# A two-layer sliding-window transformer on one core: ring, banks, masks and GLU halves rearranged

## The chip, the cores and the metric

The kernel runs on one core of one Trainium2 chip. The metric is the time of one execution on the device in microseconds; three runs of the kernel before gave a median of 736.29 us (734.07 to 737.18).

## The reference

Two layers, each of attention and a gated unit, on 2048 tokens of width 512, in bf16:

```python
x = x + A_ref(layernorm(x))     # 32 heads of 16; query i sees keys j with 0 <= i - j < 256; then @ wo
x = x + B_ref(layernorm(x))     # (sigmoid(x @ w_gate) * (x @ w_up)) @ w_down, inner width 1792
x = x + A_ref(layernorm(x))     # the same weights again
x = x + B_ref(layernorm(x))
```

## The kernel before

Tokens go in 16 tiles of 128 and 4 groups of 512. The program is fully unrolled and every engine works in the order in which it was issued. `run` (L364) writes that order: 256 slots of the attention (layer, key tile `t`, head group `g` of 4 heads, eight slots a tile), and into each slot it fills other work up to a budget `T_SLOT` of estimated TensorE nanoseconds.

A slot issues, in order: `scores` (L275), four matmuls side by side of one key tile against the three query tiles that can see it, into the one score tile of four PSUM banks, and one exponential on ScalarE into a ring in SBUF; every fourth slot `values` (L304), 48 small matmuls for one query tile and 16 heads, five slots after the first scores that it needs; the steps that have come due (`at`, L357); units of the streams; and last `mask` (L293), a multiply on VectorE for the diagonal block and a select on GpSimd for the block at the window's end. A step that follows another comes one slot later: values, two transposes with the division between them (`norm1`, `norm2`), output product (`oproj`) with the residual and the layer norm's statistics, normalising (`ln_apply`), its transpose (`ln_transpose`). All these transposes use one PSUM bank, `ps_m`; the 512-wide products use the two banks of `ps_d`.

Streams are lists of units: projections (`proj_units`, 12 units of four matmuls of 512 columns for each group) and GLU (`glu_units`, 28 such units for gate and up and 12 pieces of the down product). A unit may run when the group's four tiles are normalised and transposed, and for projections 3 and up from a free slot (L360: 58, 90, 122, 154, 186) on, since keys and values have three buffers. GLU streams go one after the other. A down product of layer 0 starts a layer norm for layer 1. GLU weights come by DMA in chunks of 128 columns, three buffers deep.

Before slot 0 the first four tiles are normalised and the whole of projection group 0 runs. `Vaug` holds each head's 16 values and a one (the sum of the softmax) at stride 18; GpSimd clears it at the start.

Of the kernel before, what the change touches and what calls it, by code (L numbers as in the profile page):

```python
# [23 lines left out]
RING_SLOTS = 7  # L24
_RING_PS = [(0, 1), (3, 1), (0, 3)]
# [7 lines left out]
T_SLOT = 2050  # L33


def ring_ps(j):
    return _RING_PS[j % 3]


def ring_slot(j, b):  # L40
    p, s = ring_ps(j)
    return p + b * s


class Net:
# [3 lines left out]
    def __init__(self, ctx, tc, A_x, wqkv, wo, w_gate, w_up, w_down, out):  # L49
# [11 lines left out]
        self.ln_st = pool("ln_st", 4)  # L61
        self.ln_xn = pool("ln_xn", 4)
        self.xnp = pool("xn_t", 3)
        self.ktp = pool("kt_tmp", 1)
# [17 lines left out]
        self.ring = big.tile([P, H, RING_SLOTS, P], BF16, name="PTring")  # L82

# [8 lines left out]
        nc.sync.dma_start(out=self.wot[:], in_=wo.rearrange("(k p) m -> p k m", p=P))  # L92
        nc.sync.dma_start(out=self.wd[:], in_=w_down.rearrange("(c p) m -> p c m", p=P))

        self.ident = big.tile([P, P], BF16, name="ident")
# [3 lines left out]
        self.nhalf = big.tile([P, 1], F32, name="nhalf")  # L99
        nc.gpsimd.memset(self.nhalf[:], -0.5)  # L100
        self.rms = [big.tile([P, 1], F32, name=f"rm{e}") for e in range(2)]
        nc.vector.memset(self.rms[0][:], 0.0)
        for m in range(4):
# [3 lines left out]
        self.maskq = big.tile([P, 4, P], BF16, name="maskq")  # L107
        nc.gpsimd.memset(self.maskq[:], 1.0)
        nc.gpsimd.affine_select(out=self.maskq[:], in_=self.maskq[:], compare_op=ALU.is_ge, fill=0.0,
                                base=0, pattern=[[0, 4], [1, P]], channel_multiplier=-1)  # L110
        for i in range(3):
            nc.gpsimd.memset(self.Vaug[i][:], 0.0)
            onesv = self.Vaug[i][:, :, 0:VS * H].rearrange("p t (h c) -> p t h c", c=VS)[:, :, :, 16:17]
            nc.gpsimd.memset(onesv, 1.0)

        self.ready = set()
        self.due = []
        self.xn = {}
# [3 lines left out]
        self.chunk_next = 0  # L122

    def ln_stats(self, key, t):
# [6 lines left out]
        nc.gpsimd.tensor_scalar(out=rs[:, 0:1], in0=mv[:, 1:2], scalar1=1e-5, scalar2=None, op0=ALU.add)  # L133
# [11 lines left out]
    def ln_later(self, key, t, first=0):  # L145

        if first:
            self.at(first, 0, lambda: self.ln_stats(key, t))
        else:
            self.ln_stats(key, t)  # L150
        self.at(first + 1, 0, lambda: self.ln_apply(key, t))
        self.at(first + 2, KT * T_TR, lambda: self.ln_transpose(key, t))

    def ln_transpose(self, key, t, bank=None):
        nc = self.nc
        tt = t % NBG
        if tt == 0:
            self.xnT[key] = self.xnp.tile([P, KT, TGW], BF16, name="xnT")
        xn = self.xn.pop((key, t))
        pt = (bank or self.ps_m).tile([P, KT, P], BF16, name="ln_tp", tag="d" if bank else "m")  # L160
        for c in range(KT):
            nc.tensor.transpose(pt[:, c, :], xn[:, c * P:(c + 1) * P], self.ident[:])  # L162
        nc.vector.tensor_copy(out=self.xnT[key][:, :, tt * P:(tt + 1) * P], in_=pt[:])  # L163
        if tt == NBG - 1:
            self.ready.add(key)
# [3 lines left out]
    def proj_units(self, L, tg):  # L169
        key = ("p", L, tg)  # L170
        b = (L * NTG + tg) % 3
        units = []
        for which in (1, 0):
            for cq in range(NCQ):
                units.append((KT * T_MM, lambda which=which, cq=cq: self._qk(key, tg, b, which, cq)))
        for tt in range(NBG):
            units.append((KT * T_MM, lambda tt=tt: self._v(key, tg, b, tt)))
        return units

    def _qk(self, key, tg, b, which, cq):  # L180
# [10 lines left out]
        if cq == 0:  # L191
            self.kt = self.ktp.tile([P, NCQ, TGW], BF16, name="kt")
        nc.scalar.copy(out=self.kt[:, cq, :], in_=pt[:])  # L193
        for e in range(2):
            nc.vector.tensor_scalar(out=self.kTp[b][:, cq, e, :], in0=self.kt[:, cq, :],
                                    scalar1=self.rms[e][:, 0:1], scalar2=None, op0=ALU.mult)
# [13 lines left out]
    def glu_units(self, L, tg):  # L210
        key = ("g", L, tg)
        units = []
        for fc in range(FC):
            units.append((KT * T_MM, lambda fc=fc: self._gate(key, L, tg, fc)))
            units.append((KT * T_MM, lambda fc=fc: self._up(key, L, tg, fc)))
        cuts = [0, 5, 10, FC]
        for tt in range(NBG):
            for a, b in zip(cuts, cuts[1:]):
                units.append(((b - a) * T_MM, lambda tt=tt, a=a, b=b: self._down(L, tg, tt, a, b)))
        return units  # L220

    def load_chunk(self):
        i = self.chunk_next
        if i >= NGI * FC:
            return
        self.chunk_next += 1
        fc = i % FC
        w = self.wgup.tile([P, KT, 2, P], BF16, name="wgu")
        self.nc.sync.dma_start(out=w[:, :, 0, :], in_=self.wg_src[:, :, fc * P:(fc + 1) * P])
        self.nc.sync.dma_start(out=w[:, :, 1, :], in_=self.wu_src[:, :, fc * P:(fc + 1) * P])  # L230
        self.chunk_w[i] = w

    def _gate(self, key, L, tg, fc):
# [12 lines left out]
    def _up(self, key, L, tg, fc):
        nc = self.nc
        w = self.chunk_w.pop((L * NTG + tg) * FC + fc)
        xnT = self.xnT[key]
        ps = self.ps_d.tile([P, TGW], F32, name="ups", tag="d")  # L250
        for kt in range(KT):
            nc.tensor.matmul(ps[:], lhsT=w[:, kt, 1, :], rhs=xnT[:, kt, :], start=(kt == 0), stop=(kt == KT - 1))  # L252
        nc.vector.scalar_tensor_tensor(out=self.hT[:, fc, :], in0=self.th[:], scalar=1.0, in1=ps[:],  # L253
                                       op0=ALU.add, op1=ALU.mult)
        if fc == FC - 1:
            del self.xnT[key]

    def _down(self, L, tg, tt, a, b):
        nc = self.nc
        t = tg * NBG + tt  # L260
# [5 lines left out]
        if b == FC:  # L266
            nc.vector.tensor_tensor(out=self.xsb[:, t, :], in0=self.xsb[:, t, :], in1=self.dps[:], op=ALU.add)
            if L == 0:
                self.ln_later(("p", 1, tg), t)
# [5 lines left out]
    def scores(self, L, t, g):  # L275
# [4 lines left out]
        pj, sj = ring_ps(t)  # L280
        kTp = self.kTp[(L * NTG + t // NBG) % 3]
        ko = (t % NBG) * P
        sps = self.ps_s.tile([P, 4, 512], F32, name="Sps")
        for m in range(4):
            nc.tensor.matmul(sps[:, m, 0:N], lhsT=kTp[32 * m:32 * m + 32, cq, e, ko:ko + P],  # L285
                             rhs=self.qT[32 * m:32 * m + 32, cq, t * P:t * P + N],
                             start=True, stop=True, tile_position=(32 * m, 0))
        h0 = 8 * cq + e
        nc.scalar.activation(out=self.ring[:, h0:h0 + 7:2, pj:pj + (nb - 1) * sj + 1:sj, :],  # L289
# [200 lines left out]
```

## Time and profile before

| | |
|---|---|
| median of 3 runs | 736.29 us |
| the profiled execution | 737.87 us |
| its span, first to last instruction | 736.1 us |
| TensorE matmuls busy, mean granted clock | 85%, 0.942 |
| VectorE, ScalarE, GpSimd busy | 62%, 62%, 30% |

The time of the profiled execution is its span and 1.8 us around it. Busy time is that of all instructions of an engine; a matmul's end is modelled. The granted clock is a share of 2.4 GHz; 0.50 is the lower level, 1.2 GHz. A stretch's mean clock tells how much of it was spent at either. In the rows PE is TensorE's matmuls, PEld its weight loads, DVE VectorE, ACT ScalarE, POOL GpSimd, and in rows of stretches they stand in this order.

### The profile page before, as it was taken

How to read it: one execution, taken by the hardware profiler on the slowest of the kernel's cores; microseconds unless marked ns; L12 is line 12 of the kernel's file. 1: busy time of each engine (PE TensorE's matmuls, PEld its weight loads, DVE VectorE, ACT ScalarE, POOL GpSimd, SP SyncE). 2: the span in 40 equal slices, each digit the busy share in tenths (PEclk: the TensorE clock that was granted, in tenths of full speed). 3: DMA queues.
4: the chain of work that ended last, by engine and by line, in shares of the span. 5: the costliest groups of instructions: out<-in, count | busy, mean ns of one | idle time of the engine just before them, and what ended most of it. 6: DMA issues, size and time to landing. Idle time of an engine off the chain costs nothing.

```text
span 736.1 us, 15556 instructions
## 1 busy us (share of the span) xinstructions
PE 628.3 (85%) x6400; PEld 281.4 (38%) x6400; DVE 459.1 (62%) x1015; ACT 456.5 (62%) x465; POOL 219.5 (30%) x367
## 2 busy tenths in 40 slices
PE   1777866998788998798897899878999999999998
PEld 1233333443333444344333344333444444444443
DVE  3376765576487767667577567758577677665232
ACT  0657866676756787455866687737877677542130
POOL 6144433233343334310233333324333333000000
PEclk9959955899999999899999899979999999999999
DMA  9300000331002311022120203200132043135260
GB/s 293 78 2 1 1 2 1 71 87 45 1 2 58 87 31 29 2 58 59 42 46 2 45 8 89 64 1 2 43 89 59 31 100 88 29 81 121 72 144 29
DMA packets 126727, 38.49 MB, mean 52 GB/s; under 512 B 118720, under 2 KB 126656, under 8 KB 126656
## 3 DMA queue, kind: packets, MB, share of 16 engines
q1 hardware_dynamic: 126656, 37.50, 21.3%
q8 instruction: 50, 0.82, 0.5%
q14 instruction: 21, 0.17, 0.1%
HBM read 35.39 MB, written 2.10 MB: 51 GB/s over the span
## 4 chain that ended last, share of the span: by engine, by line
PE 63%; DVE 21%; ACT 8%; POOL 4%; issue 3%; ACTq 0%; POOLq 0%
PE ups L252 12%; PE gps L242 12%; PE dps L264 12%; ACT PTring L289 7%; PE Sps L285 7%; PE proj_ps L186 5%; DVE ln_stats L131 4%; PE OPps L350 4%; PE OTps L314 3%; DVE xn L141 3%; DVE PTring L298 3%; PE tps L326 3%; DVE xnT L163 3%; DVE xsb L352 2%; POOL ln_rs L134 2%
## 5 line engine op out<-in xcount | busy, mean ns | idle before, releaser
L289 ACT ACTIVATE PTring<-Sps 128x1536 bf16<-128x1536 f32 (+2 forms) x256 | 351.4, 1373 | 123.0 <-PE Sps L285 105.8
L301 POOL TENSOR_SCALAR_AFFINE_SELECT PTring<-PTring 128x512 bf16<-128x512 bf16 x224 | 156.6, 708 | 229.9 <-ACT PTring L289 229.9
L298 DVE TENSOR_TENSOR PTring<-PTring,maskq 128x512 bf16<-128x512 bf16 x256 | 123.0, 481 | 36.2 <-ACT PTring L289 35.8
L253 DVE SCALAR_TENSOR_TENSOR hT<-gth,ups 128x512 bf16<-128x512 bf16 x112 | 76.8, 685 | 77.7 <-PE ups L252 60.4
L244 ACT ACTIVATE gth<-gps 128x512 bf16<-128x512 f32 x112 | 66.7, 596 | 83.4 <-PE gps L242 81.0
L252 PE MATMUL ups<-xnT,wgu 128*128 128x512 bf16 x448 | 117.5, 385 | 0.5 <-DVE hT L253 0.5
L242 PE MATMUL gps<-xnT,wgu 128*128 128x512 bf16 x448 | 117.0, 384 | 0.0
L264 PE MATMUL dps<-wd,hT 128*128 128x512 bf16 x448 | 112.3, 393 | 0.0
L285 PE MATMUL Sps<-qT,kTp 32*128 32x384 bf16 (+2 forms) x1024 | 89.6, 338 | 20.7 <-ACT PTring L289 20.5
L133 POOL TENSOR_SCALAR ln_rs<-ln_mv 128x1 f32<-128x1 f32 x64 | 18.4, 287 | 218.3 <-DVE ln_mv L132 218.3
L285 PEld LDWEIGHTS <-kTp 32*128 32x128 bf16 x1024 | 30.5, 91 | 129.2 <-issue 128.9
L186 PE MATMUL proj_ps<-xnT,wq 128*128 128x512 bf16 x256 | 67.5, 402 | 3.4 <-ACT kt L193 1.9
L162 PE MATMUL ln_tp<-ident,xn 128*128 128x128 bf16 x256 | 28.7, 242 | 45.7 <-DVE xn L141 39.9
L264 PEld LDWEIGHTS <-hT 128*128 128x128 bf16 x448 | 42.3, 101 | 45.7 <-issue 5.2
L252 PEld LDWEIGHTS <-wgu 128*128 128x128 bf16 x448 | 40.5, 99 | 48.0 <-issue 9.2
L319 DVE CAST OTs<-OTps 128x512 bf16<-128x512 f32 x64 | 44.1, 689 | 23.4 <-PE OTps L314 23.2
L242 PEld LDWEIGHTS <-wgu 128*128 128x128 bf16 x448 | 41.7, 99 | 43.4 <-issue 2.5
L314 PE MATMUL OTps<-PTring,Vaug 128*32 128x128 bf16 x2880 | 54.6, 227 | 0.0
L326 PE MATMUL tps<-ident,OTs 128*128 128x128 bf16 x256 | 26.7, 231 | 26.4 <-DVE xnT L163 26.1
L314 PEld LDWEIGHTS <-Vaug 128*32 128x32 bf16 x2880 | 43.0, 100 | 11.5 <-issue 10.4
L141 DVE TENSOR_SCALAR xn<-xsb,ln_mv,ln_rs 128x512 bf16<-128x512 bf16 x64 | 38.2, 601 | 12.8 <-POOL ln_rs L134 11.3
L131 DVE BATCH_NORM_STATS2 ln_stats<-xsb 128x6 f32<-128x512 bf16 x64 | 44.2, 691 | 3.1 <-DMA xsb<-in_A_x_dram 1.5
(37 smaller groups left out, 449.1 us busy)
## 6 DMA issues: line engine op xcount, KB each, us to landing
wgu<-in_B_w_gate_dram SPq DMA_DIRECT2D x112, 128.0 KB, 2.4
wgu<-in_B_w_up_dram SPq DMA_DIRECT2D x112, 128.0 KB, 2.8
out_dram<-xsb SPq DMA_DIRECT2D x16, 128.0 KB, 1.7
wd<-in_B_w_down_dram SPq DMA_DIRECT2D x1, 1792.0 KB, 12.6
wq<-in_A_wqkv_dram SPq DMA_DIRECT2D x3, 512.0 KB, 5.6
xsb<-in_A_x_dram SPq DMA_DIRECT2D x3, 512.0 KB, 8.4
xsb<-in_A_x_dram SPq DMA_DIRECT2D x4, 128.0 KB, 2.3
wot<-in_A_wo_dram SPq DMA_DIRECT2D x1, 512.0 KB, 8.6
```

Source lines behind the costliest of these rows:

```text
L131: nc.vector.bn_stats(out=st[:], in_=self.xsb[:, t, :])
L186: nc.tensor.matmul(pt[:], lhsT=self.wq[:, kt, c0:c0 + P], rhs=xnT[:, kt, :], start=(kt == 0), stop=(kt == KT - 1))
L242: nc.tensor.matmul(ps[:], lhsT=w[:, kt, 0, :], rhs=xnT[:, kt, :], start=(kt == 0), stop=(kt == KT - 1))
L244: nc.scalar.activation(out=self.th[:], in_=ps[:], func=AF.Tanh, scale=0.5)
L252: nc.tensor.matmul(ps[:], lhsT=w[:, kt, 1, :], rhs=xnT[:, kt, :], start=(kt == 0), stop=(kt == KT - 1))
L253: nc.vector.scalar_tensor_tensor(out=self.hT[:, fc, :], in0=self.th[:], scalar=1.0, in1=ps[:], op0=ALU.add, op1=ALU.mult)
L264: nc.tensor.matmul(self.dps[:], lhsT=self.hT[:, fc, tt * P:(tt + 1) * P], rhs=self.wd[:, fc, :], start=(fc == 0), stop=(fc == FC - 1))
L285: nc.tensor.matmul(sps[:, m, 0:N], lhsT=kTp[32 * m:32 * m + 32, cq, e, ko:ko + P], rhs=self.qT[32 * m:32 * m + 32, cq, t * P:t * P + N], s ...
L289: nc.scalar.activation(out=self.ring[:, h0:h0 + 7:2, pj:pj + (nb - 1) * sj + 1:sj, :], in_=sps[:, :, 0:N].rearrange("p w (b c) -> p w b c" ...
L298: nc.vector.tensor_tensor(out=r0, in0=r0, in1=self.maskq[:], op=ALU.mult)
L301: nc.gpsimd.affine_select(out=r2, in_=r2, compare_op=ALU.is_ge, fill=0.0, base=-1, pattern=[[0, 4], [-1, P]], channel_multiplier=1)
L314: nc.tensor.matmul(OT[32 * g:32 * g + 32, col, :], lhsT=Va[:, jj % NBG, VS * h:VS * h + 32], rhs=self.ring[:, h, ring_slot(jj, t - jj), :] ...
```

## The change

- The ring has six blocks instead of seven, by a table. Where the blocks of a key tile lie in the ring in another order than the queries, `scores` issues its matmuls in pieces, so that the exponential still writes one stepped block: one piece for every third key tile, two for the next, three for the third.
- `ps_m` is gone. `ps_d` has three banks, and all transposes take one of them; the score tile is allocated once.
- Values come six slots after the first scores that they need. Masks work on eight heads, every second slot, for the two slots before, and are issued after the slot's first unit.
- The GLU of the first group of layer 0 and of the last group of layer 1 runs as two streams of 256 tokens. A stream now needs its own tiles only. Weight chunks have 256 columns.
- K and Q products are issued in pairs, and a slot asks only for the pair that it needs (`ensure`); what it pulls in counts in the budget. Before slot 0 only the first pair runs. The budget is 2100.
- The epsilon of the layer norm is added on VectorE. K's weights are loaded before Q's; the clears of `Vaug`, now without the value columns, come after the first normalisation.

```diff
-RING_SLOTS = 7
-_RING_PS = [(0, 1), (3, 1), (0, 3)]
+RING_SLOTS = 6
+RING = [(2, 3, 1), (4, 2, 0), (3, 4, 5)]
-T_SLOT = 2050
+T_SLOT = 2100
+LN_DMA = False
...
 def ring_slot(j, b):
-    p, s = ring_ps(j)
-    return p + b * s
+    return RING[j % 3][b]
...
-        self.ktp = pool("kt_tmp", 1)
+        self.ktp = pool("kt_tmp", 2)
...
-        self.ps_s = pool("ps_s", 1, True)
+        ps_fix = pool("ps_fix", 1, True)
         self.ps_o = pool("ps_o", 1, True)
-        self.ps_d = pool("ps_d", 2, True)
-        self.ps_m = pool("ps_m", 1, True)
+        self.ps_d = pool("ps_d", 3, True)
+        self.sps = ps_fix.tile([P, 4, 512], F32, name="Sps")
...
-        for i in range(3):
+        for i in (1, 0, 2):
             nc.sync.dma_start(out=self.wq[:, :, i * D:(i + 1) * D], in_=wq_src[:, :, i * D:(i + 1) * D])
...
+    def constants(self):
+        nc = self.nc
+        for i in range(3):
+            ones = self.Vaug[i][:, :, 0:VS * H].rearrange("p t (h c) -> p t h c", c=VS)[:, :, :, 16:VS]
+            nc.gpsimd.memset(ones, 1.0)
+            nc.gpsimd.memset(self.Vaug[i][:, :, VS * H:VW], 0.0)
+            if i == 0:
+                nc.gpsimd.memset(self.maskq[:], 1.0)
...
-        nc.gpsimd.tensor_scalar(out=rs[:, 0:1], in0=mv[:, 1:2], scalar1=1e-5, scalar2=None, op0=ALU.add)
+        nc.vector.tensor_scalar(out=rs[:, 0:1], in0=mv[:, 1:2], scalar1=1e-5, scalar2=None, op0=ALU.add)
...
+            pt = self.ps_d.tile([P, KT, P], BF16, name="ln_tp", tag="d")
+            for c in range(KT):
+                nc.tensor.transpose(pt[:, c, :], xn[:, c * P:(c + 1) * P], self.ident[:])
+            nc.vector.tensor_copy(out=dst, in_=pt[:])
+        self.ready[key, t] = self.slot + (LN_LAG if LN_DMA else 1)
...
+    def _ln_rest(self, key, t):
+        if key not in self.xnT and len(self.xnT) >= 3:
+            self.at(1, 0, lambda: self._ln_rest(key, t))
+            return
+        self.ln_apply(key, t)
...
+    def glu_stream(self, L, t0, n):
+        tg = t0 // NBG
+        key = ("g", L, tg)
+        gi = L * NTG + tg
+        s = Stream(("g", L, t0), 0)
+        s.needs = [(key, t) for t in range(t0, t0 + n)]
+        w = n * P
...
         for fc in range(FC):
+            s.add(KT * (w / 2.4 + 3), None, lambda fc=fc: self._gate(key, base + fc // 2, fc, c0, w))
+            s.add(KT * (w / 2.4 + 3), None, lambda fc=fc: self._up(key, base + fc // 2, fc, c0, w, last))
...
+        f0 = (i % (FC // 2)) * 2 * P
+        w = self.wgup.tile([P, KT, 2, 2 * P], BF16, name="wgu")
+        self.nc.sync.dma_start(out=w[:, :, 0, :], in_=self.wg_src[:, :, f0:f0 + 2 * P])
+        self.nc.sync.dma_start(out=w[:, :, 1, :], in_=self.wu_src[:, :, f0:f0 + 2 * P])
...
+        while self.chunk_next < min(i + 3 - (fc % 2 == 0), self.chunks):
             self.load_chunk()
...
+        order = sorted(range(nb), key=lambda b: ring_slot(t, b))
+        p0 = ring_slot(t, order[0])
+        step = ring_slot(t, order[1]) - p0 if nb > 1 else 1
+        pieces = []
+        for i, b in enumerate(order):
+            if pieces and pieces[-1][1] + pieces[-1][2] == b:
+                pieces[-1][2] += 1
+            else:
+                pieces.append([i, b, 1])
...
+        for i, b, n in pieces:
+            for m in range(4):
+                nc.tensor.matmul(sps[:, m, i * P:(i + n) * P], lhsT=kTp[32 * m:32 * m + 32, cq, e, ko:ko + P],
+                                 rhs=self.qT[32 * m:32 * m + 32, cq, (t + b) * P:(t + b + n) * P],
+                                 start=True, stop=True, tile_position=(32 * m, 0))
...
+    def mask(self, t, cq):
+        nc = self.nc
+        r0 = self.ring[:, 8 * cq:8 * cq + 8, ring_slot(t, 0), :]
         nc.vector.tensor_tensor(out=r0, in0=r0, in1=self.maskq[:], op=ALU.mult)
+    def mask2(self, t, cq):
         if t + 2 < NT:
+            r2 = self.ring[:, 8 * cq:8 * cq + 8, ring_slot(t, 2), :]
...
     def norm1(self, L, t, half, st, OTs):
-        tps = self.ps_m.tile([P, 4, P], BF16, name="tps", tag="m")
+        tps = self.ps_d.tile([P, 4, P], BF16, name="tps", tag="d")
...
+        order = [("p", 0, 0), ("p", 0, 1), ("p", 0, 2), ("p", 0, 3), ("g", 0, 0, 2), ("g", 0, 2, 2), ("p", 1, 0),
+                 ("g", 0, 4, 4), ("p", 1, 1), ("g", 0, 8, 4), ("p", 1, 2), ("g", 0, 12, 4), ("p", 1, 3),
+                 ("g", 1, 0, 4), ("g", 1, 4, 4), ("g", 1, 8, 4), ("g", 1, 12, 2), ("g", 1, 14, 2)]
...
         for t in range(NBG):
+            self.ln_stats(k0, t)
+            if t > 0:
+                self.ln_apply(k0, t - 1)
+                self.ln_move(k0, t - 1)
+        self.ln_apply(k0, NBG - 1)
+        self.ln_move(k0, NBG - 1)
+        for t in range(NBG, 2 * NBG):
+            self.ln_stats(("p", 0, 1), t)
+        self.constants()
...
+        for tag in (("k", 0, 0), ("q", 0, 0)):
+            self.ensure(tag)
...
+                for tag in (("k", gi, g // 2), ("q", gi, g // 2), ("q", gq, g // 2)):
+                    used += self.ensure(tag)
                 self.scores(L, t, g)
...
-            v = s - 5
+            v = s - 6
...
+                used += st_.pop(self.done)
+                n += 1
+                if n == 1:
+                    self.masks(s, total)
+            if n == 0:
+                self.masks(s, total)
...
+    def masks(self, s, total):
+        if s % 2 == 0 and 2 <= s <= total:
+            g = (s - 2) % SLOTS_L
+            self.mask(g // SLOTS_T, (g % SLOTS_T) // 2)
+            self.mask2(g // SLOTS_T, (g % SLOTS_T) // 2)
```

## Rows read from the trace of the kernel before

**Rows 1.** The page: busy time of the engines, share of the span.
```profile
PE 628.3 (85%) x6400; PEld 281.4 (38%) x6400; DVE 459.1 (62%) x1015; ACT 456.5 (62%) x465; POOL 219.5 (30%) x367
```

**Rows 2.** Stretches: length, busy time and instructions by engine, clock, DMA share, GB/s.
```profile
0.00:17.42 17.42, 2.43 (x17) 1.48 (x18) 6.68 (x22) 1.28 (x1) 12.81 (x23) 1.00 0.92 290
30.91:216.32 185.41, 145.22 (x1533) 65.85 (x1532) 120.60 (x279) 128.39 (x123) 69.82 (x116) 0.83 0.09 21
96.96:119.49 22.53, 14.54 (x213) 7.82 (x213) 12.66 (x29) 14.51 (x10) 9.76 (x15) 0.50 0.00 1
216.32:660.93 444.61, 396.26 (x4433) 178.06 (x4434) 302.07 (x662) 304.95 (x306) 136.10 (x227) 0.97 0.20 47
237.81:256.05 18.24, 17.09 (x198) 7.66 (x197) 12.96 (x28) 14.53 (x15) 6.18 (x10) 1.00 0.39 88
292.48:318.60 26.12, 19.80 (x203) 8.58 (x204) 16.87 (x35) 12.11 (x10) 9.02 (x16) 0.87 0.01 2
471.21:498.19 26.98, 21.85 (x204) 9.25 (x203) 16.05 (x36) 11.61 (x9) 7.51 (x13) 0.81 0.06 13
660.93:736.10 75.17, 71.13 (x368) 30.76 (x366) 27.32 (x45) 14.93 (x25) 0.79 (x2) 1.00 0.38 91
680.00:700.00 20.00, 20.00 (x92) 8.57 (x91) 5.50 (x8) 2.39 (x4) 0.00 (x0) 1.00 0.32 80
```

**Rows 3.** Stretches, exponentials (L289) alone: length, their busy time and count, clock, DMA.
```profile
30.90:216.30 185.40, 104.63 (x72) 0.83 0.09 21
237.80:256.00 18.20, 11.58 (x8) 1.00 0.39 88
292.40:318.50 26.10, 11.61 (x8) 0.87 0.01 2
```

**Rows 4.** Waits of PE from 216.3 to 660.9: total us, times, longest us.
```profile
PE ln_tp L162 <- DVE xn L141: 20.8, 27, 1.3
PE tps L326 <- DVE xnT L163: 16.7, 24, 0.9
PE ln_tp L162 <- DVE xnT L163: 4.0, 3, 1.3
PE Sps L285 <- ACT PTring L289: 3.6, 13, 0.4
PE tps L339 <- DVE xnT L163: 3.0, 4, 0.9
```

**Rows 5.** Timeline of the head: start, us, engine, what, [idle before <-releaser].
```profile
2.51 2.12 POOL L112 MEMSET Vaug<- 128x2432 bf16 x1
2.97 0.69 DVE L131 BATCH_NORM_STATS2 ln_stats<-xsb 128x6 f32<-128x512 bf16 x1 [1.46 <-DMA xsb<-in_A_x_dram]
3.69 0.18 DVE L132 BATCH_NORM_AGGREGATE ln_mv<-ln_stats 128x2 f32<-128x6 f32 x1
10.41 0.37 POOL L133 TENSOR_SCALAR ln_rs<-ln_mv 128x1 f32<-128x1 f32 x1
11.48 0.41 DVE L141 TENSOR_SCALAR xn<-xsb,ln_mv,ln_rs 128x512 bf16<-128x512 bf16 x1 [5.23 <-POOL ln_rs L134]
12.60 0.42 DVE L163 COPY xnT<-ln_tp 128x512 bf16<-128x512 bf16 x1 [0.70 <-PE ln_tp L162]
19.94 0.62 DVE L195 TENSOR_SCALAR kTp<-kt,rm 128x512 bf16<-128x512 bf16 x2 [2.58 <-ACT kt L193]
```

**Rows 6.** Timeline of TensorE in the clean stretch.
```profile
239.59 0.85 PE L314 MATMUL OTps<-PTring,Vaug 128*32 128x128 bf16 x48
```

**Rows 7.** The page, costliest groups: busy us, mean ns | idle before, releaser.
```profile
L298 DVE TENSOR_TENSOR PTring<-PTring,maskq 128x512 bf16<-128x512 bf16 x256 | 123.0, 481 | 36.2 <-ACT PTring L289 35.8
L253 DVE SCALAR_TENSOR_TENSOR hT<-gth,ups 128x512 bf16<-128x512 bf16 x112 | 76.8, 685 | 77.7 <-PE ups L252 60.4
L244 ACT ACTIVATE gth<-gps 128x512 bf16<-128x512 f32 x112 | 66.7, 596 | 83.4 <-PE gps L242 81.0
L242 PEld LDWEIGHTS <-wgu 128*128 128x128 bf16 x448 | 41.7, 99 | 43.4 <-issue 2.5
```

More of the change, by code (lines that the diff above doesn't have):

```diff
@@ L82, in __init__ @@
         self.ring = big.tile([P, H, RING_SLOTS, P], BF16, name="PTring")
+        self.maskq = big.tile([P, 8, P], BF16, name="maskq")
+        self.ident = big.tile([P, P], BF16, name="ident")
+        self.nhalf = big.tile([P, 1], F32, name="nhalf")
+        self.rms = [big.tile([P, 1], F32, name=f"rm{e}") for e in range(2)]
         x_src = A_x[0].rearrange("(t p) d -> p t d", p=P)
@@ L106, in __init__ @@
                                 op0=ALU.mult, op1=ALU.add)
[L107 to L116, printed above, removed]
         self.due = []
+        self.done = set()
+        self.ready = {}
         self.xn = {}
@@ L143, in ln_apply, with ln_move @@
         self.xn[key, t] = xn
[L145 to L154, printed above, removed]
+    def ln_move(self, key, t):
         nc = self.nc
         tt = t % NBG
-        if tt == 0:
+        if key not in self.xnT:
@@ L158, in ln_transpose @@
             self.xnT[key] = self.xnp.tile([P, KT, TGW], BF16, name="xnT")
         xn = self.xn.pop((key, t))
[L160 to L169, printed above, removed]
-        key = ("p", L, tg)
[L171 to L175, printed above, removed]
-        for tt in range(NBG):
-            units.append((KT * T_MM, lambda tt=tt: self._v(key, tg, b, tt)))
-        return units
+        dst = self.xnT[key][:, :, tt * P:(tt + 1) * P]
@@ L268, in _down @@
             if L == 0:
[L269 removed]
+                self.ln_later(("p", 1, t // NBG), t)
             else:
@@ L284, in scores @@
[L284 to L287, printed above, removed]
+        sps = self.sps
+        for i, b, n in pieces:
[3 more added lines that the diff above has]
+                                 start=True, stop=True, tile_position=(32 * m, 0))
@@ L335, in norm2 @@
+    def norm2(self, L, t, half, st, ov):
         nc = self.nc
-        tps2 = self.ps_m.tile([P, 2, P], BF16, name="tps2", tag="m")
-        ov = On[:].rearrange("p c g x -> p (c g x)")
+        tps2 = self.ps_d.tile([P, 2, P], BF16, name="tps2", tag="d")
         for c in range(2):
@@ L374, in run, with next_stream @@
+    def next_stream(self):
+        glu = False
+        for s in self.streams:
+            if not s.units:
+                continue
+            g = s.name[0] == "g"
+            if g and glu:
+                continue
+            glu = glu or g
+            if self.slot >= s.free_slot and all(self.ready.get(n, 1 << 30) <= self.slot for n in s.needs):
+                return s
+        return None
+    def run(self):
         nc = self.nc
         self.slot = 0
-        for t in range(NBG):
-            self.ln_stats(("p", 0, 0), t)
@@ L389, in run @@
-        done = set()
-        def next_stream():
-            for s in streams:
-                if s[1] and s[0] in self.ready and self.slot >= s[2]:
-                    if s[0][0] == "g":
-                        prev = [r for r in streams if r[0][0] == "g" and r[1] and r is not s]
-                        if prev and streams.index(prev[0]) < streams.index(s):
-                            continue
-                    return s
-            return None
-        states = {}
+        self.chunks = 0
```

216 lines of the change are left out of this document (123 added, 93 removed).

## Prediction

> **What bounds the kernel now.** I read the engines' totals first, then stretches cut at the exponentials (one per slot, so they are the kernel's clock), and then the waits in each stretch. TensorE is busy 85% of the span [rows 1]; the other three have a third or more to spare. But that share is a mean over four stages [rows 2, 3].
>
> The head ends with the exponential of slot 0 at 30.91 us. Slots 0 to 71 (72 exponentials) take 185.4 us, 2.58 a slot, at a clock of 0.83; ten of them ran at 0.50, half of full speed, with TensorE busy 14.5 of 22.5 us: there was nothing to fill them with. The other 184 slots, 72 to 255, take 444.6 us, 2.42 a slot. Their clean form is the eight slots from 237.81: 18.24 us, 2.28 a slot, TensorE busy 94%. Two stretches of the down products of layer 0 stand out, 26.1 us for eight slots and 27.0 us for the other, at a clock of 0.87 and 0.81. The tail of 75.2 us is TensorE's own, busy 71.1.
>
> What stops TensorE in slots 72 to 255 is short and names itself [rows 4]: 20.8 us for a normalised tile from VectorE, and 16.7, 4.0 and 3.0 us where a transpose waits for the copy out of the earlier transpose. Those last three are the one bank `ps_m`, 23.7 us in 31 waits. The chain through the exponential costs 3.6 us there: it is no bound in this stage.
>
> **Head: 30.9 becomes 18.5.** GpSimd clears the three value tiles first (2.12 us each and more), so its first step for a tile whose statistics were done at 3.87 starts at 10.41 [rows 5]. The change puts these clears behind the four tiles. Per tile VectorE then has statistics 0.69, aggregate 0.18, the added sum (an operation on one column: between 0 and the aggregate's 0.18; I take 0.15, near the aggregate), 0.41 to normalise, 0.70 waiting for the transposes, 0.42 to copy: 2.55. Four from 2.97 make 13.2 instead of 17.4. Then come the four added statistics (4 x 1.02 = 4.1, on VectorE, in front of the keys' scaling), the scaling 0.62, and about 0.6 to scores and exponential: 18.5. The K and Q products of quarter 0 fit under those statistics. On the weights' load, K now comes before Q, so nothing new waits there. Gain 12.4. It is not all free: ten units of projection group 0 move into slots 0 to 5, of four matmuls of 0.217 us each (20.00 us of a busy TensorE over 92 [rows 2]), 0.87 a unit.
>
> **Slots 0 to 71: 185.4 becomes 168.** By the budgets of the diff (2100 a slot, 370 for scores, 864 a full unit, 439 a half-width one) I count which slots find a unit. Before, 21 don't: 0 to 5 and 23 to 37. After: the values of tile 1 end in slot 18, its output product in 21, its transpose in 23, so the first half GLU runs from slot 24 to 36, the second from 40 to 53, projection group 3 from its free slot 58 to 65; empty are 37 to 39, 54 to 57 and 66 to 71, 13 slots. From slot 72 on both plans have a unit always, since tile 7 allows the next GLU in slot 70 before and 72 after. So the two kernels have the same work behind them at slot 72, and the gain so far is plain. Prices: 13 empty slots at 2.25 (22.53 us over 10) are 29.2. The other 59 at the clean 2.28, less 0.09 for bank waits and plus 0.03 for pieces (both below), 2.22, are 131.2. The 12 down units of layer 0 have the excess of one such stretch, 26.1 - 18.2 = 7.9, of which I leave half: 4. The first slots at half clock: 4. Together 168.4.
>
> **Slots 72 to 255: 444.6 becomes 422.6.** Bank waits: transposes now take the next of three banks. All 23.7 us could go; what is late next is the evacuation of a matmul bank, so I take two thirds: -16. Wait for the normalised tile: the epsilon step moves from GpSimd to VectorE, and VectorE does half as many mask multiplies, on keys two slots old rather than this slot's, so it no longer stands behind an exponential. A multiply takes 0.48 us [rows 7]; for twice the columns it is between 0.48 and 0.96, so 128 of them free VectorE of 0 to 61 us, on the path only where VectorE is late. From 0 to -20.8; I take a third, -7. Half clock: 0.13 of 26.1 and 0.19 of 27.0 us lost; with fewer stalls about half returns, -4.
>
> Score pieces: of three successive key tiles one keeps four matmuls, one has eight, one twelve. Leaving out the last tiles of a layer that makes 15 added pieces per layer and slot of a row, 240 in all, 168 of them here. The columns stay the same; a piece adds four loads and starts. The nearest row is the values: 48 matmuls of 128 columns in 0.85 us, 0.071 per four [rows 6], where four side by side stream 128 columns in about 0.054 (a quarter of 0.217). Lower end 0.01 a piece; upper end 0.10, one load not hidden (99 ns, [rows 7]). I take 0.03: +5.
>
> *A rule against it.* While TensorE was busy 20.00 of 20.00 us, 91 weight loads lay wholly beside matmuls [rows 2], each for all 128 rows. The Trainium skill (TensorE: Matmul & The Clock Gate, Part 3, The mechanism) says that a weight load overlaps running matmuls only when it goes to another row group. A second piece reloads the same four row groups, so by the rule it would pay its load, 240 x 0.1 = 24 us by the row above. These 91 loads disagree with it in that form, so it stays a rival.
>
> The ring of six slots: each block is overwritten two slots after its last reader, and TensorE takes both in order, so no new wait. Values one slot later find masks that were issued two slots before. The fixed score tile changes nothing while it is single before and after. Half-width GLU: 224 added loads of 99 ns beside matmuls of 108 ns (half of 0.217): 0 to 22 us, I take +0 here; tanh and product of a pair take at most what they took for the full width, 0.60 and 0.69 [rows 7], against 0.87 of TensorE, so they are hidden at either end.
>
> **Tail: 75 stays 75.** The plan leaves 61 us of products after slot 255 against 62. The last half GLU no longer waits for four tiles, but TensorE was never short there. Weights come in 512 KB chunks, one per 1.75 us, 300 GB/s. Before, 80 GB/s took a share of 0.32, so 250 at most with packets of half the length; the head reached 290 with long ones [rows 2]. At 250 a chunk is 0.35 us late: from 0 to 14 x 0.35 = 5 us; I take 2, against 1 less work and 1 of stalls.
>
> **Sum.** 18.5 + 168.4 + 422.6 + 75.2 = 684.7 of span; the profiled execution took 737.87 for a span of 736.1, so 686.5; the median lies 1.6 below that execution: about **685**.
>
> **Rivals.**
> *More comes back (662).* Bank waits and tile waits go whole: 23.7 + 20.8 instead of 23, 22 less. For it: the masks leave VectorE's queue. Against it: VectorE is busy 302 of 444.6 us there, more in the down stretches.
> *The waits change their name (708).* Three banks now serve matmul outputs too; where VectorE is late, a transpose, or a product, waits all the same. The 23 us of slots 72 to 255 stay; the head and the filling remain.
> *Loads exposed (704).* 240 pieces at 0.10 instead of 0.03 are +17, and two more in the half-width products.
> *Slower (over 740).* One mechanism: a bank that a transpose holds until VectorE has read it is missing to the next product. Some 632 tiles pass the three banks (96 projection, 280 GLU, 64 down and output, 192 transposes). Before, the bank shared by 192 transposes cost 23.7 us, 0.12 each; at that price for all 632 it is +78, 763. It decides from 0.09 a tile. Against it: matmul products had two banks and waited almost never [rows 4]; now there are three, and transposes are short.
> *It doesn't do what it says (735).* The early start is eaten by the ten moved units, 8.7 us, and the pieces.
>
> **Chances.** Forecast 0.55 (its own range 668 to 702), more 0.11, waits renamed 0.16, loads exposed 0.07, slower 0.07, nothing 0.04. Range: from just under the second case to past the third and fourth, 657 to 716. About 0.5% is what a measurement of this kernel can tell from no change. Faster 0.88, same 0.04, slower 0.08.
>
> **What would show it.** Right: first exponential near 18.5 us; the clock at full through slots 24 to 53; slot 72 near 187; in the list of TensorE's waits no transpose behind an earlier copy above 8 us in slots 72 to 255; a score group of two or three pieces under 0.1 us longer. Wrong: a new large wait of products for VectorE or ScalarE (banks), loads between pieces with TensorE idle, a slot price above 2.35 in clean rows, or gaps for weights in the tail. The forecast fails altogether if slot 72 comes after 205 us.

## The result, and the profile after

| | before | after |
|---|---|---|
| median | 736.0 us (734.07 to 737.18, 4 runs) | 695.27 us (691.66 to 696.94, 4 runs) |
| profiled execution, span | 737.87, 736.1 us | 694.75, 693.0 us |
| mean granted clock | 0.942 | 0.963 |

After is 0.944 of before, interval 0.940 to 0.949: 41 us faster, where 51 were forecast. By stages of the profiled executions, in us:

| | before | forecast | after |
|---|---|---|---|
| first exponential starts | 30.9 | 18.5 | 17.6 |
| slots 0 to 71 | 185.4 | 168.4 | 175.1 |
| slots 72 to 255 | 444.6 | 422.6 | 423.7 |
| tail | 75.2 | 75.2 | 76.7 |
| span | 736.1 | 684.7 | 693.0 |

These are the stretches of the kernel after (called "after" from here on), with the columns of [rows 2]. The last three are eight slots each, at the three down products of layer 0 that fall into slots 72 to 255.

```profile
0.00:17.57 17.57, 6.34 (x32) 2.67 (x33) 11.72 (x41) 2.45 (x3) 5.44 (x16) 1.00 0.92 290
17.57:192.63 175.06, 147.60 (x1988) 79.63 (x1987) 122.12 (x281) 134.58 (x147) 54.81 (x65) 0.93 0.21 58
192.63:616.30 423.67, 400.02 (x5103) 182.70 (x5103) 288.69 (x601) 306.72 (x309) 103.58 (x112) 0.97 0.18 51
616.30:693.00 76.70, 66.39 (x464) 39.09 (x462) 28.95 (x60) 15.50 (x36) 0.55 (x1) 1.00 0.41 117
264.89:285.29 20.40, 17.57 (x261) 8.51 (x262) 17.35 (x38) 13.06 (x11) 8.16 (x10) 1.00 0.07 18
337.39:362.31 24.92, 20.19 (x217) 8.88 (x215) 16.46 (x36) 11.60 (x8) 5.83 (x7) 0.85 0.01 1
435.71:461.06 25.35, 18.21 (x233) 8.18 (x231) 17.85 (x37) 12.09 (x9) 7.98 (x9) 0.86 0.00 1
```

The clock of slots 0 to 71 rose from 0.83 to 0.93: that of slots 24 to 53 from 0.73 to 0.95, while that of slots 54 to 71 fell from 1.00 to 0.82. That of slots 72 to 255 stayed at 0.97. The down stretches were three before as well; to the 26.1 and 27.0 us of [rows 2] comes

```profile
390.29:415.77 25.48, 18.97 (x184) 8.42 (x185) 16.41 (x35) 12.69 (x10) 9.70 (x17) 0.87 0.05 11
```

After, the first takes 20.4 us at full clock, and the other two still take 25, at 0.85 and 0.86. A clean eight slots, cut at the exponentials as in [rows 3], went from 18.2 us (slots 80 to 87) to 17.3 (slots 88 to 95):

```profile
17.50:192.60 175.10, 104.89 (x72) 0.93 0.21 58
229.60:246.90 17.30, 11.68 (x8) 1.00 0.22 63
```

The waits of TensorE from 192.6 to 616.3, against [rows 4]:

```profile
PE ln_tp L178 <- DVE xn L162: 7.7, 19, 1.4
PE tps L408 <- DVE On L393: 4.2, 10, 0.9
PE Sps L337 <- ACT PTring L341: 2.2, 8, 0.4
PE tps L383 <- DVE OTs L371: 2.2, 2, 1.1
PE ln_tp L178 <- DVE On L393: 1.9, 1, 1.9
PE ups L295 <- DVE On L393: 1.8, 1, 1.8
PE gps L284 <- DVE hT L297: 1.4, 4, 0.8
```

No transpose waits for the copy of an earlier one any more (`xnT` stands nowhere on the right). Products, and once a transpose (`ln_tp` behind `On`), wait for a bank in rows of 1 to 2 us. What is left besides is a transpose that waits for its own input from VectorE. In the tail two rows of a new kind stand:

```profile
PE ups L295 <- DMA wgu<-in_B_w_up_dram: 3.4, 6, 1.4
PE gps L284 <- DMA wgu<-in_B_w_gate_dram: 2.4, 3, 0.9
```

The page's costliest groups show the masks of eight heads and the normalising, to be held against [rows 7]:

```profile
L353 POOL TENSOR_SCALAR_AFFINE_SELECT PTring<-PTring 128x1024 bf16<-128x1024 bf16 x112 | 123.5, 1106 | 183.6 <-ACT PTring L341 178.0
...
L348 DVE TENSOR_TENSOR PTring<-PTring,maskq 128x1024 bf16<-128x1024 bf16 x128 | 90.3, 706 | 0.0
...
L162 DVE TENSOR_SCALAR xn<-xsb,ln_mv,ln_rs 128x512 bf16<-128x512 bf16 x64 | 47.1, 744 | 3.6 <-POOL ln_rs L155 3.4
```

The multiply for twice the columns takes 706 ns, not 962, and never waits for an exponential, as foreseen. But the normalising, which the change does not touch, takes 744 ns. In the page of before it is

```profile
L141 DVE TENSOR_SCALAR xn<-xsb,ln_mv,ln_rs 128x512 bf16<-128x512 bf16 x64 | 38.2, 601 | 12.8 <-POOL ln_rs L134 11.3
```

so each of the 64 takes 0.14 us longer.

### The profile page after: what moved, and what is told of

The parts are those of the page before. It is cut to its first block, busy times and chain, and to the rows that moved or that the text cites. A ratio compares the mean times of both kernels' runs of the same rounds, so it can differ in the third digit from the quotient of the medians.

```text
span 693.0 us, 17643 instructions
## 1 busy us (share of the span) xinstructions
PE 620.3 (90%) x7584; PEld 304.1 (44%) x7584; DVE 451.5 (65%) x979; ACT 459.3 (66%) x493; POOL 164.4 (24%) x191
## 4 chain that ended last, share of the span: by engine, by line
PE 60%; DVE 23%; ACT 7%; issue 5%; DMA 3%; POOL 1%; SPq 0%; POOLq 0%; ACTq 0%
PE ups L295 11%; PE gps L284 11%; PE dps L307 10%; PE Sps L337 7%; PE proj_ps L224 5%; ACT PTring L341 5%; PE OTps L366 5%; DVE xn L162 4%; PE OPps L419 4%; DVE ln_stats L152 4%; DMA wgu<-in_B_w_up_dram 3%; DVE OTs L371 3%; DVE PTring L348 2%; PE v_ps L240 2%; DVE hT L297 2%
## 5 line engine op out<-in xcount | busy, mean ns | idle before, releaser
L353 POOL TENSOR_SCALAR_AFFINE_SELECT PTring<-PTring 128x1024 bf16<-128x1024 bf16 x112 | 123.5, 1106 | 183.6 <-ACT PTring L341 178.0
L297 DVE SCALAR_TENSOR_TENSOR hT<-gth,ups 128x512 bf16<-128x512 bf16 (+1 forms) x140 | 81.1, 579 | 82.1 <-PE ups L295 57.2
L295 PE MATMUL ups<-xnT,wgu 128*128 128x512 bf16 (+1 forms) x560 | 123.3, 344 | 8.2 <-DMA wgu<-in_B_w_up_dram 3.4
L284 PE MATMUL gps<-xnT,wgu 128*128 128x512 bf16 (+1 forms) x560 | 123.6, 344 | 4.9 <-DMA wgu<-in_B_w_gate_dram 2.4
L287 ACT ACTIVATE gth<-gps 128x512 bf16<-128x512 f32 (+1 forms) x140 | 71.1, 512 | 84.7 <-PE gps L284 81.7
L155 POOL TENSOR_TENSOR ln_rs<-ln_rs,nhalf 128x1 f32<-128x1 f32 x64 | 38.3, 598 | 282.5 <-DVE ln_rs L154 277.3
L337 PE MATMUL Sps<-qT,kTp 32*128 32x128 bf16 (+2 forms) x1984 | 87.7, 249 | 16.5 <-ACT PTring L341 13.3
L348 DVE TENSOR_TENSOR PTring<-PTring,maskq 128x1024 bf16<-128x1024 bf16 x128 | 90.3, 706 | 0.0
L295 PEld LDWEIGHTS <-wgu 128*128 128x128 bf16 x560 | 52.2, 99 | 47.8 <-issue 9.7
L284 PEld LDWEIGHTS <-wgu 128*128 128x128 bf16 x560 | 52.1, 100 | 43.8 <-issue 7.6
L178 PE MATMUL ln_tp<-ident,xn 128*128 128x128 bf16 x256 | 26.7, 233 | 26.1 <-DVE xn L162 23.8
L310 DVE TENSOR_TENSOR xsb<-xsb,dps 128x512 bf16<-128x512 bf16 x32 | 21.9, 685 | 31.6 <-PE dps L307 31.4
```

What stands on the lines that cost most here:

```text
L284: nc.tensor.matmul(ps[:, 0:w], lhsT=wt[:, kt, 0, (fc % 2) * P:(fc % 2 + 1) * P], rhs=xnT[:, kt, c0:c0 + w], start=(kt == 0), stop=(kt == K ...
L295: nc.tensor.matmul(ps[:, 0:w], lhsT=wt[:, kt, 1, (fc % 2) * P:(fc % 2 + 1) * P], rhs=xnT[:, kt, c0:c0 + w], start=(kt == 0), stop=(kt == K ...
L297: nc.vector.scalar_tensor_tensor(out=self.hT[:, fc, 0:w], in0=self.th[:, 0:w], scalar=1.0, in1=ps[:, 0:w], op0=ALU.add, op1=ALU.mult)
L337: nc.tensor.matmul(sps[:, m, i * P:(i + n) * P], lhsT=kTp[32 * m:32 * m + 32, cq, e, ko:ko + P], rhs=self.qT[32 * m:32 * m + 32, cq, (t + ...
L348: nc.vector.tensor_tensor(out=r0, in0=r0, in1=self.maskq[:], op=ALU.mult)
L353: self.nc.gpsimd.affine_select(out=r2, in_=r2, compare_op=ALU.is_ge, fill=0.0, base=-1, pattern=[[0, 8], [-1, P]], channel_multiplier=1)
```

## The experiments

All are the kernel after with one edit (one joins three of them), except the last, which is the kernel before with one edit. Every ratio is to the kernel before, with its interval. Stages are given as first exponential / slots 0 to 71 / slots 72 to 255 / tail; after is 17.6 / 175.1 / 423.7 / 76.7.

**One bank for the transposes again.**

```diff
-        self.ps_d = pool("ps_d", 3, True)
+        self.ps_d = pool("ps_d", 2, True)
+        self.ps_m = pool("ps_m", 1, True)
...
-            pt = self.ps_d.tile([P, KT, P], BF16, name="ln_tp", tag="d")
+            pt = self.ps_m.tile([P, KT, P], BF16, name="ln_tp", tag="m")
```

(and the same for `tps` and `tps2`)

> The changed kernel with its banks undone: all transposes share one bank of their own again and the products have two. Theory (the third bank took away the waits of a transpose for the copy out of the earlier one): these waits come back, some 20 us of TensorE idle in slots 72 to 255 and some 8 before, so 710 to 722 us. Rival (the masks moved out of VectorE's queue are what shortened these waits, the copy is now early enough): at most 8 us more, 695 to 703, and the waits behind an xnT copy sum to less than 8 us.

Measured 754.96 us, 1.025 (1.021 to 1.030), 17.7 / 199.5 / 456.9 / 78.8: the rest of the change without the third bank is slower than before. It costs 60 us, more than any theory said. TensorE's waits of the whole span:

```profile
PE ln_tp L179 <- DVE On L394: 55.7, 32, 3.1
PE ln_tp L179 <- DVE xn L163: 14.9, 10, 5.4
...
PE ln_tp L179 <- DVE xnT L180: 6.4, 7, 2.6
```

The first row is the one bank: the transpose of a normalised tile, issued behind `norm1`'s transpose, does not start until the division has read that out. With the third row and two smaller ones (3.1 and 2.0 us) the waits behind the bank are 67 us; the second row is a wait for the transpose's own tile.

**Is it the order?** The same kernel, with the move of the normalised tile issued ahead of `norm1`:

```diff
-            self.at(1, KT * T_TR, lambda: self.ln_move(key, t))
+            self.due.insert(0, [self.slot + 1, KT * T_TR, lambda: self.ln_move(key, t)])
```

> The kernel with one transpose bank (e1) and, in a slot where both come due, the layer norm's transpose issued ahead of the transpose of the values, as the kernel before had it. Theory (the 60 us of e1 are a bank held by the values' transpose through VectorE's reciprocal and multiply while the layer norm's transpose stands behind it; the other way round it is held only through a copy): the 55.7 us of waits of that transpose go, 20 to 30 us of waits for an xnT copy come in their place, 712 to 730 us. Rival (one bank is short by itself, whatever the order): 745 us or more.

Measured 749.22 us, 1.021 (1.017 to 1.025), 17.6 / 194.8 / 454.2 / 78.8. The waits change their name:

```profile
PE ln_tp L179 <- DVE xn L163: 43.0, 41, 5.5
PE tps L384 <- DVE xnT L180: 27.1, 32, 2.2
```

The second row, with two smaller ones (5.9 and 2.1 us), is the bank, 35 us instead of 67. The first is not: the transpose, now earlier in the slot, waits for its own tile. So the order does not give the 60 us back, as the rival had it. How much of them one bank would cost in an order without that new wait, this run does not show.

**The old head.** All clears before the first norm, and all of projection group 0 before slot 0:

```diff
+        self.constants()
         for t in range(NBG):
...
-        for tag in (("k", 0, 0), ("q", 0, 0)):
+        for tag in [u[1] for u in self.streams[0].units]:
             self.ensure(tag)
```

(with `constants` clearing the value columns too, and its later call taken out)

> The changed kernel with its head undone: the value tiles are cleared whole, and the masks built, before the first normalisation, and all twelve units of projection group 0 run before slot 0. Theory (the early start is worth what it saves less the ten units that it moves into slots 0 to 5): the first exponential comes 12 to 14 us later and slots 0 to 5 take 4 to 5 us less, so 702 to 706 us. Rival (the early start is eaten by the moved units): 695 to 698.

Measured 709.7 us, 0.965 (0.961 to 0.969), 33.5 / 181.4 / 419.8 / 76.4. The head is worth 14 us, more than either expectation said. Slots 0 to 71 should have become shorter with ten units less in them, and took 6 us more, at a clock of 0.87 instead of 0.93. So the moved units did not eat the early start. Why the lower clock falls there is open.

**Always one piece per query tile.** 896 matmuls more, 224 pieces:

```diff
-            if pieces and pieces[-1][1] + pieces[-1][2] == b:
+            if False:
```

> The changed kernel with every score group in as many pieces as it has query tiles: 240 pieces more again (for key tiles with two or one piece, three). Theory (the second piece's loads are hidden, 0.00 to 0.03 us a piece): 0 to 7 us more, 695 to 702. Rival (a load to the same row groups is exposed, 0.10 us a piece): 24 us more, 715 to 722.

Measured 692.27 us, 0.941 (0.938 to 0.945), 17.7 / 176.1 / 420.2 / 75.7. Pieces cost nothing that can be measured; the rival of exposed loads falls. The trace of after says the same. From the start of a score group to the start of the next operation, at full clock and with no wait between, the median is 0.273 us for groups of four matmuls (85 of them), 0.276 for eight (66) and 0.279 for twelve (66). Two rows of its timeline of TensorE, a group of twelve and, elsewhere, one of four:

```profile
343.87 0.35 PE L337 MATMUL Sps<-qT,kTp 32*128 32x128 bf16 x12
344.15 0.40 PE L383 MATMUL tps<-ident,OTs 128*128 128x128 bf16 x4
...
229.18 0.34 PE L337 MATMUL Sps<-qT,kTp 32*128 32x384 bf16 x4
229.45 0.28 PE L408 MATMUL tps<-ident,On 128*128 128x128 bf16 x2
```

The next operation starts 0.28 us after the start of the twelve and 0.27 us after that of the four.

**Whole GLU groups at both ends.**

```diff
-        ... ("g", 0, 0, 2), ("g", 0, 2, 2), ("p", 1, 0),
+        ... ("g", 0, 0, 4), ("p", 1, 0),
...
-        ... ("g", 1, 12, 2), ("g", 1, 14, 2)]
+        ... ("g", 1, 12, 4)]
```

> The changed kernel with whole GLU groups of four tiles at both ends. Theory (the half groups fill the early slots, and what they do there is missing behind slot 255): by the plan's budgets 14 slots more without a unit before slot 72, six slots' work more after 255, 11 us, against 6 us of waits for weights that leave the tail: 698 to 704 us. Rival (TensorE's work is the bound and the early filling is worth nothing): 689 to 695, the waits for weights gone.

Measured 690.54 us, 0.938 (0.934 to 0.943), 17.8 / 167.5 / 432.4 / 74.0. The halves are worth nothing; the median without them is 5 us lower, though the intervals meet. They fill early slots at 7.6 us, save 8.7 later, and lose 2.7 in the tail, whose two rows of weight waits are gone without them. The clock tells the same: with whole groups it is 0.82 in slots 24 to 53 and 1.00 in slots 54 to 71, with halves 0.95 and 0.82.

**Masks of four heads, in every slot.** As in the kernel before, at the end of a slot for its own heads (`mask2` in the same way):

```diff
-        if s % 2 == 0 and 2 <= s <= total:
-            g = (s - 2) % SLOTS_L
-            self.mask(g // SLOTS_T, (g % SLOTS_T) // 2)
+        if s < total:
+            g = s % SLOTS_L
+            self.mask(g // SLOTS_T, g % SLOTS_T)
```

> The changed kernel with its masks undone: four heads at a time, at the end of every slot, for the slot's own scores. Theory (masks of two slots before no longer hold up VectorE behind an exponential, and there are half as many): TensorE's waits for a normalised tile in slots 72 to 255 go back from 7.7 us toward 20.8, and VectorE has some 30 us more to do: 705 to 715 us. Rival (the banks and the epsilon on VectorE did it): 693 to 699.

Measured 681.72 us, 0.927 (0.923 to 0.931), 17.8 / 175.7 / 412.1 / 74.7: 13.5 us faster than after. My theory that the large masks help is wrong in sign. The multiplies wait for an exponential again, 23.2 us on the page, and it harms nothing, while the normalising is short:

```profile
L348 DVE TENSOR_TENSOR PTring<-PTring,maskq 128x512 bf16<-128x512 bf16 x256 | 121.4, 474 | 25.5 <-ACT PTring L341 23.2
...
L162 DVE TENSOR_SCALAR xn<-xsb,ln_mv,ln_rs 128x512 bf16<-128x512 bf16 x64 | 35.8, 565 | 2.3 <-POOL ln_rs L155 2.3
```

**Small masks, issued late.** Four heads in every slot, for the slot before, after the first unit. This keeps the place of the changed kernel and undoes the size.

```diff
-        if s % 2 == 0 and 2 <= s <= total:
-            g = (s - 2) % SLOTS_L
+        if 1 <= s <= total:
+            g = (s - 1) % SLOTS_L
```

> The changed kernel with masks of four heads in every slot, for the slot before, at the place where the change issues them (after the slot's first unit). It separates the size of the masks from their place. Theory (what cost 13 us is the size: one operation of 0.7 us on VectorE and one of 1.1 us on GpSimd, during which the normalising on VectorE takes 0.74 us instead of 0.57): about as fast as with the old masks, 680 to 686 us. Rival (the place in the middle of the slot puts them in front of the division and the copies): 690 to 696.

Measured 686.8 us, 0.935 (0.931 to 0.938), 17.6 / 173.8 / 415.3 / 76.2, on the border between the two expectations. Of the 13.5 us some 8.5 go with the size and 5 with the place.

**A fourth chunk buffer.**

```diff
-        self.wgup = pool("wgu", 3)
+        self.wgup = pool("wgu", 4)
...
-        while self.chunk_next < min(i + 3 - (fc % 2 == 0), self.chunks):
+        while self.chunk_next < min(i + 4 - (fc % 2 == 0), self.chunks):
```

> The changed kernel with four weight buffers instead of three, and chunks asked for one chunk earlier. Theory (in the tail a chunk of 512 KB asked for two chunks ahead comes late by its latency): the 5.8 us of TensorE waiting for weights in the tail fall under 2, 690 to 693 us. Rival (the transfer rate is the bound, 300 GB/s asked of engines that give less with such packets): the waits stay at 4 to 6 us, 694 to 697.

Measured 688.12 us, 0.935 (0.932 to 0.939), 17.8 / 175.9 / 420.0 / 70.4. Of the tail's 5.8 us of weight waits 0.7 are left:

```profile
PE ups L295 <- DMA wgu<-in_B_w_up_dram: 0.7, 2, 0.5
```

The chunks came late because they were asked for late, and not because the queue could bring no more.

**One slot more between a step and its transposes.**

```diff
-            self.at(1, KT * T_TR, lambda: self.ln_move(key, t))
+            self.at(2, KT * T_TR, lambda: self.ln_move(key, t))
```

(and the same for `norm1` and `norm2`)

> The changed kernel with one slot more between each step and the transposes that follow it (normalised tile, values, division). Theory (the waits that are left, TensorE in front of a transpose whose data VectorE has not finished, are latency, in the down stretches of layer 0 above all): they fall from 22 to under 8 us in slots 72 to 255, the two stretches of 25 us go to 20, half of the drops of the clock go: 678 to 688 us. Rival (VectorE and GpSimd lack throughput there): no less than 692; and since every GLU becomes ready three slots later, perhaps 2 to 4 us more.

Measured 662.1 us, 0.899 (0.895 to 0.902), 17.8 / 168.9 / 414.9 / 60.7: 33 us below after. The stretches:

```profile
17.80:186.60 168.80, 145.18 (x1983) 79.28 (x1983) 119.09 (x273) 135.27 (x146) 54.26 (x62) 0.96 0.21 59
186.60:601.50 414.90, 401.41 (x5171) 187.48 (x5170) 292.72 (x610) 309.73 (x315) 104.53 (x112) 0.99 0.19 56
601.50:662.20 60.70, 52.62 (x402) 33.43 (x401) 24.98 (x57) 11.35 (x29) 1.10 (x2) 1.00 0.43 122
```

The slots hold 63 matmuls more and are 15 us shorter all the same, so the tail has 52.6 us of products instead of 66.4. In the list of TensorE's waits from 186.6 to 601.5 transposes are left with two waits, of 0.3 and 0.2 us. Its first rows are

```profile
PE Sps L337 <- ACT PTring L341: 5.4, 13, 1.6
PE dps L307 <- DVE OnT L410: 1.9, 2, 1.3
```

**Is it the filling?** A larger budget, so that slots take more products without the lag:

```diff
-T_SLOT = 2100
+T_SLOT = 2130
```

> The changed kernel with a slot's budget of 2130 instead of 2100. A slot with both transposes due stands at 826 after them; a unit makes 1690, and a second needs 1690 + 432 = 2122 within the budget. By the plan 20 us of products move from behind slot 255 into the slots. Theory (13 units in eight slots instead of 12 fill TensorE's idle time, which is half of what the kernel with one slot more of lag gained): the tail is 18 to 21 us shorter, the slots 5 to 10 us longer, 680 to 688 us. Rival (the slots grow by what moves into them): 692 to 697.

Measured 698.05 us, 0.949 (0.946 to 0.952), 17.8 / 182.4 / 440.5 / 52.2. The tail loses 24.5 us and the slots take 24 more. Packing alone moves work; it is not what the lag gains. With the lag, all the rows of TensorE's waits over the span sum to 51 us instead of 67, and the mean clock is 0.982 instead of 0.963; how the 33 us divide between the two is not shown.

**Small masks, fourth buffer and lag together.** The edits of those three.

> The changed kernel with the old masks (e5), one slot more between a step and its transposes (e7) and four weight buffers (e6) together. Theory (their gains of 14, 33 and 7 us touch different waits): 641 to 652 us. Rival (the masks and the lag both remove the same thing, TensorE waiting for a late VectorE): 655 to 661.

Measured 659.16 us, 0.897 (0.894 to 0.899), 17.6 / 168.4 / 413.2 / 56.5. It is the fastest that was run, and not to be told from the lag alone. The fourth buffer still shows in the tail (56.5 for 60.7, weight waits of 1.2 us for 4.6). The small masks do not: TensorE's waits for a normalised tile over the whole span are 10.0 us, and 10.4 with the lag alone. The lag had already removed what they remove.

**The third bank alone, in the kernel before.**

```diff
-        self.ps_d = pool("ps_d", 2, True)
-        self.ps_m = pool("ps_m", 1, True)
+        self.ps_d = pool("ps_d", 3, True)
```

(all transposes from `ps_d`)

> The kernel before with one part of the change alone: no bank for transposes of their own, three banks for products and transposes. Theory of the prediction (the bank's worth is the waits that it shows, 23.7 us in slots 72 to 255 of which 16 come back, and some 13 us before slot 72): 708 to 720 us. Rival one (the bank is worth in this kernel what it is worth in the changed one, 55 to 60 us): 676 to 681. Rival two (the waits change their name, VectorE is late all the same): 728 to 736.

Measured 687.69 us (6 runs), 0.937 (0.933 to 0.940), 30.0 / 167.9 / 413.8 / 72.9: the bank alone gives 47.5 us, and the whole change 41. Its two stretches of slots and, from 197.9 to 611.7, its waits, numbered by its own lines:

```profile
30.03:197.90 167.87, 135.54 (x1516) 63.47 (x1532) 119.76 (x279) 128.36 (x123) 70.71 (x116) 0.89 0.10 23
197.90:611.68 413.78, 378.90 (x4385) 174.99 (x4434) 299.05 (x662) 304.75 (x306) 135.13 (x227) 1.00 0.22 50
```
```profile
PE ln_tp L161 <- DVE xn L140: 20.8, 30, 1.3
...
PE tps L325 <- DVE xnT L162: 1.4, 2, 0.7
```

In slots 72 to 255 the bank's rows went from 23.7 to 1.4 us, the wait for the normalised tile stayed at 20.8, and the clock rose from 0.97 to 1.00: 30.8 us less. Slots 0 to 71 lost 17.5 with the old head and all 21 empty slots.

## Why the prediction was right, and where by luck

The time came out inside the forecast's own range, and of the stages the head and slots 72 to 255 within 1.1 us. The sum held better than its terms, and that was luck. In slots 72 to 255 the terms were -16 for the bank, -7 for the normalised tile, -4 for the clock and +5 for the pieces. The runs give 30.8 us less for the bank in the kernel before (with the clock that came back), 11.6 more for the large masks (423.7 with them, 412.1 with small ones), and nothing for the pieces.

Of the signs, transposes behind an earlier copy are gone (below 8 us was asked), and a score group of twelve is 0.006 us longer than one of four (below 0.1). Slot 72 came at 192.6 us for 187, and the clock of slots 24 to 53 was 0.95, not full.

**Head: right.** 30.9 to 17.6 for a forecast of 18.5. Per tile the normalised tiles follow each other by 2.45 us (2.55 worked out):

```profile
4.95 0.40 DVE L162 TENSOR_SCALAR xn<-xsb,ln_mv,ln_rs 128x512 bf16<-128x512 bf16 x1
...
7.41 0.40 DVE L162 TENSOR_SCALAR xn<-xsb,ln_mv,ln_rs 128x512 bf16<-128x512 bf16 x1
...
9.86 0.40 DVE L162 TENSOR_SCALAR xn<-xsb,ln_mv,ln_rs 128x512 bf16<-128x512 bf16 x1
```

Put back, the old head costs 14 us in all.

**Banks: right mechanism, size too small.** I took 16 us in slots 72 to 255 and 5 before them, 21 together; alone the bank is worth 47.5. Two things failed. I read the list of waits for slots 72 to 255 alone and gave slots 0 to 71 the same price per slot. Their own list in the trace of before has 12.7 us of it:

```profile
PE Sps L285 <- ACT PTring L289: 16.9, 21, 1.8
PE tps L326 <- DVE xnT L163: 9.5, 10, 2.6
...
PE tps L339 <- DVE xnT L163: 1.8, 2, 1.3
PE ln_tp L162 <- DVE xnT L163: 1.4, 1, 1.4
```

And I discounted the rows by a third for what would be late next, where 23.7 and 12.7, 36.4 us, came back whole and more: with them went lower-clock stretches (mean clock 0.942 to 0.970). It is not always more: in the changed kernel the rows behind one bank sum to 67 us, and the third bank gave 60.

**Masks: wrong sign.** They stood in the -7 for the normalised tile. That row did fall, from 20.8 to 7.7 us, but it falls to 5.7 with small masks too, so the large ones are not its cause; the epsilon's move to VectorE was not run by itself. I priced VectorE's multiply alone. The pieces of work that the change lengthened are the multiply (0.48 to 0.71 us), the select on GpSimd (0.71 to 1.11 us), and the normalising where it runs beside a select. In a down stretch of after the timeline shows one case:

```profile
346.63 2.18 POOL L353 TENSOR_SCALAR_AFFINE_SELECT PTring<-PTring 128x1024 bf16<-128x1024 bf16 x2
346.80 1.06 DVE L162 TENSOR_SCALAR xn<-xsb,ln_mv,ln_rs 128x512 bf16<-128x512 bf16 x1
...
346.94 0.28 PE L408 MATMUL tps<-ident,On 128*128 128x128 bf16 x2 [0.83 <-DVE On L393]
...
347.92 0.61 PE L178 MATMUL ln_tp<-ident,xn 128*128 128x128 bf16 x4 [0.69 <-DVE xn L162]
```

The normalising takes 1.06 us beside two selects in a row, and TensorE, in order behind it, stands 0.69 us. Small masks in the old place are worth 13.5 us, 8.5 of them by their size. That the overlap with GpSimd is the whole of it is not shown: no run took the selects away.

**Filling by half GLUs: credited, and worth nothing.** The drop of slots 0 to 71 was put down to 13 empty slots in place of 21 and came out near (175.1 for 168.4). But whole groups give 167.5 there, and the kernel before with the third bank and its 21 empty slots 167.9. A product moved from a later slot to an earlier one saves time in the slot that it leaves and costs time in the slot that it enters, and only the difference is gained. Here that was nothing, and the larger budget shows the same.

**Pieces, and the rule against them.** I took +5; it is 0, the lower end. The rule of the Trainium skill (TensorE: Matmul & The Clock Gate, Part 3, The mechanism), that a weight load overlaps running matmuls only when it goes to another row group, does not hold here, taken by itself: 224 pieces more on the same row groups left the time where it was. The same section of the Trainium skill also lets a load run ahead of matmuls into a background weight buffer, which the prediction left out.

**Tail: 76.7 for 75.2.** Weights were late by 5.8 us, not 2: the term's upper end of 5 was a rate, and the cause is how far ahead a chunk is asked for.

**Rivals.** "Slower", by banks that products miss, is refuted by the list of waits. "Loads exposed" fell with the pieces. "Waits change their name" is true in part (22 us of waits instead of 48, the largest for VectorE's input). "More comes back" had the bank right and the masks wrong. "It doesn't do what it says" falls with the old head, which costs 14 us.

Put together from single edits, the 41 us are some -47.5 for the bank and -14 for the head, against +13.5 for the masks and +5 to +7 for the halves and their late chunks (these two overlap). That this comes out near 41 is no proof, since the edits do not simply add: with the 60 us that the bank is worth in the changed kernel, it would be some 54. Three things stay open. One bank costs 60 us in the changed kernel and 47.5 in the one before: more waits stand behind it there (67 us for 36.4), and their order alone does not mend that. The low clock in slots 0 to 71 with the old head has no explanation. And the epsilon on VectorE, the extra slot of the values, the K and Q pairs and the step of the budget from 2050 to 2100 were not run by themselves.

## What to carry to other kernels

Where an in-order engine waits for one shared buffer, read the list of its waits for every stage, and expect about their sum back (here 47.5 us for 36.4 listed, and 60 for 67). Then give dependent steps room before filling idle time: one slot of lag ahead of the transposes gave 33 us, and packing the slots fuller gave none. An edit that halves a count of instructions by doubling their length can lengthen the delays of all that stands behind them, so it has to be tried alone.

## What the runs showed of the hardware

VectorE's normalising takes 0.41 us where no select of GpSimd runs (mean of 23 rows of the kernel with masks of four heads in every slot), and 0.65 beside one (41 rows, up to 0.86); beside the selects of eight heads it is 0.93 (37 rows of after, up to 1.18). The same tile and operation thus take twice as long by what another engine does.

The rows also show how. Two cases of after, each a select and the normalising beside it:

```profile
209.51 1.09 POOL L353 TENSOR_SCALAR_AFFINE_SELECT PTring<-PTring 128x1024 bf16<-128x1024 bf16 x1
210.05 0.70 DVE L162 TENSOR_SCALAR xn<-xsb,ln_mv,ln_rs 128x512 bf16<-128x512 bf16 x1
...
333.88 1.09 POOL L353 TENSOR_SCALAR_AFFINE_SELECT PTring<-PTring 128x1024 bf16<-128x1024 bf16 x1
333.95 1.16 DVE L162 TENSOR_SCALAR xn<-xsb,ln_mv,ln_rs 128x512 bf16<-128x512 bf16 x1
```

Both end 0.14 to 0.15 us after their select. So do all 33 rows of after in which a select was running when the normalising began; in the 4 rows in which the normalising began first, it took 0.40 to 0.41. So it is not slowed by a share: it ends with the select, and a longer select holds it longer.

The Trainium skill (GPSIMD Engine Reference, 1. Specifications) says that GpSimd shares its way to SBUF with VectorE and that some of VectorE's instructions contend for it; these rows agree, and give the price that this section does not.
